# A tile of 128 bytes becomes 256: what stands behind it in SBUF moves from remainder 32 to remainder 160 by 256

## The chip, the cores and the metric

The kernel runs on one core of a Trainium2 chip. The metric is the device time of one execution in microseconds (us), the median of several runs. The profile's span goes from the first to the last instruction of one execution that the hardware profiler recorded.

## What is computed

Two stages. The first is a short convolution over the sequence whose weights come with each token (softmax over 7 taps, 8 heads of 24 channels); the second is a feed-forward layer with ELU between its two products, over 16384 tokens, 192 channels and 2048 inner channels.

```python
w = softmax(weight_gen, axis=-1)                  # [4, 4096, 8, 7]
x_unf = x_pad[:, idx, :].reshape(B, S, 7, 8, 24)  # the token and the 6 before it
x = einsum('bshk,bskhg->bshg', w, x_unf).reshape(16384, 192)
h = x @ w_in                                      # [16384, 2048]
g = where(h > 0, h, exp(min(h, 0)) - 1)
out = g @ w_out                                   # [16384, 192]
```

All is float32. The weights arrive as 64-bit words and are decoded on the chip.

## The kernel before

The 16384 tokens are worked on in 32 blocks of 512. Of each block the convolution is made by GpSimd (products and sums, lines 508 and 524), transposed by VectorE (629), and split into a high and a low part (xhi, xlo; lines 637 and 639), which SyncE's copies also bring to the other half of the partitions (657). Line 473 is the exponential of the softmax; wm and ws (lines 469 to 479) hold its maximum and its sum, 32 numbers a partition each.

The products run on TensorE in fp32r, one pass, with high and low parts. One step is one block and one k of 8, which stands for two tiles of 128 inner channels:

- h = x @ w_in, line 685 (`product_in`): for each of the two tiles nine products, (w high, x high), (w low, x high), (w high, x low) for three thirds of the channels. w_in's tile WI is loaded as weights, 64 partitions by 128 columns, and x's part is the moving stream, 512 columns. The two tiles use the lower and the upper 64 partitions, one instruction each, and run side by side.
- ELU, lines 742, 744, 747, 752, 754: ScalarE and VectorE take h from PSUM and leave its high part hi and its low part lo in SBUF.
- out += g @ w_out, line 713 (`product_out`): here ELU's parts are the weights (64 by 128), and w_out's tile WO is the stream: 384 columns (high and low part) for hi, 192 for lo. Again one instruction for each half of the partitions, side by side. The sums lie in acc and accd in PSUM.

Two steps' products with w_in (36 instructions) stand behind one another, and then two earlier steps' products with w_out (64 instructions). All of block 0 (`plain`) is worked on in plain fp32 in place of that, four passes, straight from the decoded weights m_in and m_out and without low parts; each such matmul stands as two records in the trace. Line 566 sums products of the convolution for blocks 0 and 1 with an identity matrix.

The order of every engine's instructions is fixed by a planner (`Plan`) that has a cost for each task, due times and a table of shifts; it does not know of addresses. TensorE waits for ELU's parts, ELU for h; h has four banks of PSUM, each of which is free again when ELU's last subtraction (754) has read it.

SBUF is filled in the order of first use, each tile at a multiple of 32 bytes. A ring of buffers lies in one piece. In bytes a partition, in the kernel before:

```
start          remainder by 256   tile (buffers x bytes)
16512           128               ident (1 x 512)
17056           160               WI, w_in's parts (1 x 24576)
41632           160               WO, w_out's parts (1 x 24576)
66208           160, 32, 160      wg (3 x 896)
68896            32               xw (3 x 5376)
85024            32               wm (1 x 128)
85152           160               ws (1 x 128)
85280            32               raw_in (3 x 6144), then v, raw_out, pa, pb
132896           32               xhi (2 x 9216)
151328           32               m_in (3 x 3072), then e, m_out
174368           32               hi (7 x 2048)
188704           32               xt (1 x 3072)
191776           32               xlo (2 x 9216)
210208           32               lo (7 x 2048)
224544           32               xc (1 x 3072)
```

Of the kernel before, what the change touches and what calls it, by code (L numbers as in the profile page):

```python
# [52 lines left out]
class Plan:  # L53
# [13 lines left out]
    def add(self, engine, cost, run, reads=(), writes=(), due=None, port=False):  # L67
        t = Task(engine, cost, run, due, port or engine == "pool")
        for h in reads:
            t.needs.update(h.writers)  # L70
        for h in writes:
            t.needs.update(h.users)
            if not h.users:
                if h.make:
                    t.makes.append(h)
                if h.before:
                    t.needs.update(h.before.users)
        for h in (*reads, *writes):
            h.users.append(t)
        for h in writes:  # L80
            h.writers.append(t)
        t.needs.discard(t)
        t.at = len(self.tasks)
        self.tasks.append(t)
        return t
# [50 lines left out]
def conv_elu_kernel(  # L136
# [12 lines left out]
    P, T, HK = weight_gen.shape  # L149
# [7 lines left out]
    H = HK // K // Q  # L157
# [5 lines left out]
    J = N // (A * S)  # L163
# [38 lines left out]
    def rows(ap, t0, n):  # L202

        return ap.rearrange("(a r) t d -> r a t d", r=R)[t0 // T][:, t0 % T:t0 % T + n]

    def quadrants():

        return [(slice((s * Q + q) * A, (s * Q + q + 1) * A), s, q)
                for s in range(S) for q in range(Q)]
# [21 lines left out]
    def ring(name, shape, bufs, dtype=F32, pool=sb):  # L231
        return Ring(pool, shape, dtype, name, bufs)
# [4 lines left out]
    r_m_out = ring("m_out", [P, 2, D], 5, I32)  # L237
    r_xw = ring("xw", [P, HALO + J, DQ], 3)
    r_wg = ring("wg", [P, J, H, K], 3)
    r_wm = ring("wm", [P, J, H, 1], 1)  # L240
    r_ws = ring("ws", [P, J, H, 1], 1)
    r_pa = ring("pa", [P, J, H, G], 2)
    r_pb = ring("pb", [P, J, H, G], 1)
# [26 lines left out]
    def act(cols, psum=False):  # L270
        return cols / 1.2 + (70 if psum else 110)

    def dve(cols):
        return cols / 0.96 + 70
# [9 lines left out]
    def dma(packets, byts):  # L284
        return packets * max(9 + byts / 12, 22) / 20
# [7 lines left out]
    def due1(k):  # L293
        if k < len(FIRST):
            return T0 + FIRST[k]
        return T0 + FIRST[-1] + (k - len(FIRST) + 1) * STEP
# [131 lines left out]
    def chunk(blk):  # L428

        n, t0 = J, blk * J * S  # L430
        xw, wg, wm, ws = r_xw.new(), r_wg.new(), r_wm.new(), r_ws.new()
        wg_h[blk] = wg
        xw_h[blk] = xw
        k, kk = n * H, n * H * K

        def w():
            return wg.t[:, 0:n]

        def wide(h):
            return h.t.to_broadcast([P, n, H, K])  # L440

        def load(to, src, n, d, at=0, both=False, only=quadrants()):
            def run():
                for p, s, q in only:
                    eng = nc.scalar if both and q else nc.sync
                    eng.dma_start(out=to()[p], in_=rows(src, t0 + s * J + at, n)[  # L446
                        :, :, q * d:(q + 1) * d])
            return run

        def load_w(only=quadrants()):  # L450
            return load(lambda: w().rearrange("p t h k -> p t (h k)"), weight_gen, n, H * K,
                        both=blk == 0, only=only)

        if blk == 0:
            add("dma", 700 + Q * S * ISSUE // 2, load_w(), writes=[wg], due=-2)
        for one in quadrants() if blk else ():
            add("dma", max(dma(A * n, H * K * 4), ISSUE), load_w([one]), writes=[wg])
        if blk == 0:
            xw_h[blk] = xw = [xw, Handle()]
            m = n + HALO  # L460
            for i, (a, b) in enumerate(((0, m - JH), (m - JH, m))):
                add("dma", dma(P * (b - a), DQ * 4),
                    load(lambda a=a, b=b: xw[0].t[:, a:b], x, b - a, DQ, a),
                    writes=[xw[i]], due=-1 + i)
        else:
            for one in quadrants():
                add("dma", max(dma(A * (n + HALO), DQ * 4), ISSUE),
                    load(lambda: xw.t, x, n + HALO, DQ, only=[one]), writes=[xw])
        add("dve", dve(kk), lambda: nc.vector.tensor_reduce(
            out=wm.t[:, :, :, 0], in_=w(), axis=AX.X, op=ALU.max), reads=[wg], writes=[wm])  # L470
        add("dve", dve(kk), lambda: nc.vector.tensor_tensor(
            out=w(), in0=w(), in1=wide(wm), op=ALU.subtract), reads=[wm], writes=[wg], port=True)
        add("act", act(kk), lambda: nc.scalar.activation(
            out=w(), in_=w(), func=ACTF.Exp), writes=[wg])
        add("dve", dve(kk), lambda: nc.vector.tensor_reduce(
            out=ws.t[:, :, :, 0], in_=w(), axis=AX.X, op=ALU.add), reads=[wg], writes=[ws])
        add("act", act(k), lambda: nc.scalar.activation(
            out=ws.t, in_=ws.t, func=ACTF.Copy, bias=1e-9), writes=[ws])
        add("dve", 6.4 * k + 60, lambda: nc.vector.reciprocal(out=ws.t, in_=ws.t),
            writes=[ws])  # L480
        if blk == 0:
            wb_h[blk] = [r_h.new(), r_h.new()]
            for i, h in enumerate(wb_h[blk]):
                def half(t, i=i):
                    return t[:, i * JH:(i + 1) * JH]

                def bank(h=h):
                    return h.t[:, 0:kk // 2].rearrange("p (t h k) -> p t h k", h=H, k=K)

                add("dve", dve(kk // 2), lambda half=half, bank=bank: nc.vector.tensor_tensor(  # L490
                    out=bank(), in0=half(w()), in1=half(wide(ws)), op=ALU.mult),
                    reads=[ws, wg], writes=[h], port=True, due=due1(0) - 14000 + 1000 * i)
                if OWN[blk][i] < K:
                    add("act", act(kk // 2, True), lambda half=half, bank=bank: nc.scalar.copy(
                        out=half(w()), in_=bank()), reads=[h], writes=[wg])
            return
        add("dve", dve(kk), lambda: nc.vector.tensor_tensor(  # L497
            out=w(), in0=w(), in1=wide(ws), op=ALU.mult), reads=[ws], writes=[wg], port=True)
# [384 lines left out]
    with tc.manual_schedule():  # L883

        nc.vector.memset(scratch, 0.0)
        add("act", 1500, lambda: nc.scalar.activation(out=scratch, in_=scratch, func=ACTF.Exp),
            due=2500)
        make_identity(nc, ident)
        turn_over(14)
        for s in range(len(todo) + LAG):  # L890
            now = todo[s] if s < len(todo) else None
            up = todo[s - LAG] if s >= LAG else None
            if now:
                blk, k = now
                if k == 0:
                    chunk(blk)
                    if blk < 2:
                        summed(blk, s, OWN[blk])
                    else:
                        conv(blk, s)  # L900
                if blk == 0:
                    if k in in_pieces:
                        weights_in(k, in_pieces[k])
                    weights_out(k)
            period(s, now, up)
            if up and up[1] == NP - 1:
                drain(up[0], s)
        plan.issue()
# [34 lines left out]
```

## Time and profile before

| | |
|---|---|
| median of 3 runs | 1163.75 us (1163.24 to 1163.84) |
| span of the profiled execution | 1161.3 us |
| the profiled execution's own time | not given apart from its span; the median is 2.45 us above it |
| TensorE busy (products) | 1154.9 us, 99% |
| ScalarE, VectorE, GpSimd busy | 913.7, 847.7, 698.3 us |
| granted TensorE clock, mean | 0.999 |
| share of the chain that ended last | PE 98% |

A busy share says that an instruction of the engine was under way, not that the engine ran at its best: products are pipelined, and the start of one and the start of the next say more than the duration of one. The chain that ended last is followed back from the last instruction, at each step to what released it. In the timeline, neighbouring instructions of a kind are merged, and the count stands behind the x; a pair that runs side by side counts as two.

### The profile page before, as it was taken

Reading aid. Unit: us, or ns where it says so; the run is one execution under the profiler, and the core shown is the slowest. Engines: PE = TensorE matmul, PEld = TensorE weight load, DVE = VectorE, ACT = ScalarE, POOL = GpSimd, SP = SyncE. Lnnn points to the kernel's source line nnn. Section 1 sums busy time; section 2 is a strip of 40 time slices with the busy share of each in tenths; the row PEclk is TensorE's granted clock in tenths of the full one; section 3 lists DMA queues with packets and bytes.
Section 4 is the critical chain, followed back from the end, with each engine's and each line's share of the span. In section 5 each row is a group of like instructions: output and inputs, shape, how many; then the busy total and the mean of one; then the engine's idle time right before and its main releaser. Section 6 shows DMA issues by size and latency. Waiting matters only on the chain.

```text
span 1161.3 us, 32341 instructions
## 1 busy us (share of the span) xinstructions
PE 1154.9 (99%) x12844; PEld 1048.7 (90%) x12844; DVE 847.7 (73%) x1502; ACT 913.7 (79%) x1794; POOL 698.3 (60%) x424
## 2 busy tenths in 40 slices
PE   9999999999999999999999999999999999999998
PEld 6699999999989989989999998998999999999997
DVE  7977768776767777777776677776777776777664
ACT  6778778787778878777878777887777887787775
POOL 4666874846687777865557755567755567653000
PEclk9999999999999999999999999999999999999999
DMA  8831322331233232213332223331223321111100
GB/s 194 165 69 43 65 65 67 71 70 43 57 66 74 49 79 54 59 43 69 70 70 49 47 46 70 71 70 40 53 49 70 70 65 35 26 31 42 42 16 15
DMA packets 143127, 71.04 MB, mean 61 GB/s; under 512 B 98816, under 2 KB 141824, under 8 KB 142976
## 3 DMA queue, kind: packets, MB, share of 16 engines
q1 hardware_dynamic: 142112, 68.72, 27.0%
q8 instruction: 101, 1.65, 0.6%
q14 instruction: 50, 0.41, 0.1%
q10 hardware_dynamic: 864, 0.25, 0.1%
HBM read 31.98 MB, written 12.58 MB: 38 GB/s over the span
## 4 chain that ended last, share of the span: by engine, by line
PE 98%; SPq 1%; DMA 0%; ACT 0%; issue 0%; DVE 0%; DVEq 0%; ACTq 0%
PE h L685 46%; PE accd L713 25%; PE acc L713 25%; PE accd L566 0%; PE acc L566 0%; SPq L446 0%; DMA raw_in<-in_moe_w_in 0%; SPq L369 0%; PE h L681 0%; ACT xhi L646 0%; DVE raw_out L867 0%; ACT acc L329 0%; ACT raw_in L332 0%; SPq L404 0%; ACT raw_out L861 0%
## 5 line engine op out<-in xcount | busy, mean ns | idle before, releaser
L747 DVE SCALAR_TENSOR_TENSOR h<-e,h 128x512 f32<-128x512 f32 x496 | 321.8, 693 | 279.8 <-ACT e L744 278.9
L742 ACT ACTIVATE e<-h 128x512 f32<-128x512 f32 x512 | 280.4, 600 | 171.5 <-PE h L685 171.3
L685 PE MATMUL h<-xhi,WI 64*128 64x512 f32 x2976 | 392.5, 394 | 0.0
L754 DVE TENSOR_TENSOR lo<-h,hi 128x512 fp32r<-128x512 f32 x496 | 326.4, 688 | 14.5 <-ACT hi L752 0.7
L752 ACT CAST hi<-h 128x512 fp32r<-128x512 f32 x496 | 290.7, 587 | 53.9 <-DVE h L747 41.2
L685 PEld LDWEIGHTS h<-xhi,WI 64*128 64x128 f32 x2976 | 279.1, 185 | 48.5
L713 PE MATMUL accd<-WO,hi 64*128 64x384 f32 x1984 | 305.9, 357 | 0.0
L713 PE MATMUL acc<-WO,hi 64*128 64x384 f32 x1984 | 304.6, 355 | 0.0
L524 POOL TENSOR_TENSOR pa<-pa,pb 128x768 f32<-128x768 f32 x150 | 289.9, 1932 | 17.0 <-DVE pb L508 5.5
L744 ACT ACTIVATE e<-e 128x512 f32<-128x512 f32 x512 | 297.9, 637 | 0.9
L508 POOL TENSOR_TENSOR pb<-xw,wg 128x768 f32<-128x768 f32 (+1 forms) x179 | 278.0, 1553 | 11.7
L713 PE MATMUL acc<-WO,lo 64*128 64x192 f32 x1984 | 255.6, 249 | 0.0
L713 PE MATMUL accd<-WO,lo 64*128 64x192 f32 x1984 | 254.8, 248 | 0.0
L508 POOL TENSOR_TENSOR pa<-xw,wg 128x768 f32<-128x768 f32 (+1 forms) x31 | 47.2, 1524 | 305.3 <-DVE wg L497 289.3
L685 PE MATMUL h<-xlo,WI 64*128 64x512 f32 x1488 | 214.6, 390 | 0.0
L713 PEld LDWEIGHTS acc<-WO,lo 64*128 64x128 f32 x1984 | 198.5, 187 | 4.6
L713 PEld LDWEIGHTS acc<-WO,hi 64*128 64x128 f32 x1984 | 196.3, 185 | 4.8
L713 PEld LDWEIGHTS accd<-WO,lo 64*128 64x128 f32 x1984 | 198.8, 188 | 0.1
L713 PEld LDWEIGHTS accd<-WO,hi 64*128 64x128 f32 x1984 | 195.1, 184 | 0.1
L685 PEld LDWEIGHTS h<-xlo,WI 64*128 64x128 f32 x1488 | 144.5, 184 | 28.2
L524 POOL TENSOR_TENSOR xc<-pa,pb 128x768 f32<-128x768 f32 x30 | 55.5, 1851 | 2.4
L639 DVE TENSOR_TENSOR xlo<-xt,xhi 128x768 fp32r<-128x768 f32 (+1 forms) x32 | 37.9, 1184 | 1.0
(84 smaller groups left out, 487.1 us busy)
## 6 DMA issues: line engine op xcount, KB each, us to landing
xw<-in_x SPq DMA_DIRECT2D x124, 168.0 KB, 3.5
xhi<-xhi SPq DMA_DIRECT2D x62, 192.0 KB, 3.0
xlo<-xlo SPq DMA_DIRECT2D x62, 192.0 KB, 2.9
out_dram<-raw_out SPq DMA_DIRECT2D x124, 96.0 KB, 1.9
wg<-in_weight_gen SPq DMA_DIRECT2D x126, 28.0 KB, 2.2
raw_out<-in_moe_w_out SPq DMA_DIRECT2D x8, 384.0 KB, 6.2
raw_in<-in_moe_w_in SPq DMA_DIRECT2D x12, 192.0 KB, 5.3
raw_in<-in_moe_w_in SPq DMA_DIRECT2D x8, 96.0 KB, 2.9
```

Of the source, the lines that this page charges most:

```text
L508: lambda: eng.tensor_tensor(out=h.t[:, 0:J], in0=xw.t[:, j0 + k:j0 + k + J, :].rearrange("p j (h g) -> p j h g", g=G), in1=wg.t[:, j0:j0 + ...
L524: add("pool", pool(J * DQ), lambda b=b, to=to: nc.gpsimd.tensor_tensor(out=to.t, in0=a.t, in1=b.t, op=ALU.add), reads=[b] if to is a else ...
L639: add("dve", dve(C * n * A), lambda i=i: nc.vector.tensor_tensor(out=to(xlo, i), in0=xt(i), in1=to(xhi, i).bitcast(F32), op=ALU.subtract), ...
L685: return lambda: nc.tensor.matmul(out=h.t, lhsT=w_in_f[k][1]()[p, c] if w is None else WI[p, k, w, c], rhs=x.t[p, c, c0:c0 + 2].rearrange( ...
L713: return nc.tensor.matmul(out=to(), lhsT=src.t[p, g * P:(g + 1) * P], rhs=w, start=start, stop=False, skip_group_check=True).ins
L742: add("act", act(N, True), lambda: nc.scalar.activation(out=e.t, in_=h.t, func=ACTF.Relu, scale=-1.0), reads=[h], writes=[e])
L744: add("act", act(N), lambda: nc.scalar.activation(out=e.t, in_=e.t, func=ACTF.Exp, scale=-1.0), writes=[e])
L747: add("dve", dve(N), lambda: nc.vector.scalar_tensor_tensor(out=to.t, in0=e.t, scalar=-1.0, in1=h.t, op0=ALU.add, op1=ALU.max), reads=[e, ...
L752: add("act", act(N, True), lambda: nc.scalar.copy(out=hi.t, in_=h.t), reads=[h], writes=[hi])
L754: add("dve", dve(N), lambda: nc.vector.tensor_tensor(out=lo.t, in0=h.t, in1=hi.t.bitcast(F32), op=ALU.subtract), reads=[h, hi], writes=[lo])
```

## The change

The tile wm gets twice the size, and the code uses its first half. All tiles that are placed behind it start 128 bytes later; WI, WO, wg and xw stay. ws stands at 32 then, and raw_in, v, raw_out, pa, pb, xhi, m_in, e, m_out, hi, xt, xlo, lo and xc at 160.

```diff
-    r_wm = ring("wm", [P, J, H, 1], 1)
+    r_wm = ring("wm", [P, 2 * J, H, 1], 1)
...
-        xw, wg, wm, ws = r_xw.new(), r_wg.new(), r_wm.new(), r_ws.new()
+        xw, wg, wm, ws = r_xw.new(), r_wg.new(), r_wm.new(lambda t: t[:, 0:J]), r_ws.new()
```

## Rows read from the trace of the kernel before

**Rows 1.** The page: busy time of the engines; granted clock in 40 slices.

```profile
PE 1154.9 (99%) x12844; PEld 1048.7 (90%) x12844; DVE 847.7 (73%) x1502; ACT 913.7 (79%) x1794; POOL 698.3 (60%) x424
...
PEclk9999999999999999999999999999999999999999
```

**Rows 2.** The page: the chain that ended last, by engine and by line.

```profile
PE 98%; SPq 1%; DMA 0%; ACT 0%; issue 0%; DVE 0%; DVEq 0%; ACTq 0%
PE h L685 46%; PE accd L713 25%; PE acc L713 25%; PE accd L566 0%; PE acc L566 0%; SPq L446 0%; DMA raw_in<-in_moe_w_in 0%; SPq L369 0%; PE h L681 0%; ACT xhi L646 0%; DVE raw_out L867 0%; ACT acc L329 0%; ACT raw_in L332 0%; SPq L404 0%; ACT raw_out L861 0%
```

**Rows 3.** The chain in order of time, 159 to 178 us: start us, us, what.

```profile
159.85 4.21 PE h L685 x36
164.05 1.14 PE acc L713 x16
165.19 1.15 PE accd L713 x16
166.33 1.15 PE acc L713 x16
167.48 1.15 PE accd L713 x16
168.63 4.21 PE h L685 x36
```

**Rows 4.** Timeline of PE, 602.7 to 604.5 us: start us, us, instruction, count.

```profile
602.99 0.34 PE L713 MATMUL acc<-WO,hi 64*128 64x384 f32 x2
603.17 0.25 PE L713 MATMUL acc<-WO,lo 64*128 64x192 f32 x2
603.26 0.36 PE L713 MATMUL acc<-WO,hi 64*128 64x384 f32 x2
603.46 0.25 PE L713 MATMUL acc<-WO,lo 64*128 64x192 f32 x2
```

**Rows 5.** Timeline of the weight loads (PEld), the same stretch.

```profile
603.17 0.19 PEld L713 LDWEIGHTS acc<-WO,hi 64*128 64x128 f32 x2
603.28 0.19 PEld L713 LDWEIGHTS acc<-WO,lo 64*128 64x128 f32 x2
603.46 0.19 PEld L713 LDWEIGHTS acc<-WO,hi 64*128 64x128 f32 x2
```

**Rows 6.** Groups by line, whole span: count, busy us, mean ns, idle before.

```profile
L685 PE MATMUL h<-xhi,WI 64*128 64x512 f32 x2976 | 392.5, 394 | 0.0
L713 PE MATMUL accd<-WO,hi 64*128 64x384 f32 x1984 | 305.9, 357 | 0.0
L713 PE MATMUL acc<-WO,hi 64*128 64x384 f32 x1984 | 304.6, 355 | 0.0
...
L685 PE MATMUL h<-xlo,WI 64*128 64x512 f32 x1488 | 214.6, 390 | 0.0
```

**Rows 7.** Lines 473 and 508: durations in ns, least/median/most; forms.

```profile
L473 ACT ACTIVATE wg<-wg x32: 388/389/424, 4.8 to 1024.6; 128x224 f32<-128x224 f32 x32
...
L508 POOL TENSOR_TENSOR pb<-xw,wg x179: 864/1546/2153, 9.1 to 1051.0; 128x768 f32<-128x768 f32 x177, 128x384 f32<-128x384 f32 x2
...
L508 POOL TENSOR_TENSOR pa<-xw,wg x31: 862/1545/1550, 8.3 to 1031.2; 128x768 f32<-128x768 f32 x30, 128x384 f32<-128x384 f32 x1
```

**Rows 8.** Timelines of DVE, PE and ACT, 607.6 to 612 us.

```profile
607.54 1.35 DVE L754 TENSOR_TENSOR lo<-h,hi 128x512 fp32r<-128x512 f32 x2
...
609.68 0.40 PE L685 MATMUL h<-xhi,WI 64*128 64x512 f32 x2
...
609.88 1.09 ACT L742 ACTIVATE e<-h 128x512 f32<-128x512 f32 x2 [1.72 <-PE h L685]
```

**Rows 9.** Timeline of PE in block 0, 31.6 to 34.6 us.

```profile
31.61 0.32 PE L713 MATMUL accd<-m_out,hi 64*128 64x192 f32 x1
...
31.77 0.32 PE L713 MATMUL accd<-m_out,hi 64*128 64x192 f32 x1
...
31.94 2.74 PE L685 MATMUL h<-xhi,m_in 64*128 64x512 f32 x12
34.51 0.32 PE L713 MATMUL accd<-m_out,hi 64*128 64x192 f32 x1
```

**Rows 10.** Timeline, 602.35 to 602.70 us: stream and next load.

```profile
602.30 0.62 PE L685 MATMUL h<-xlo,WI 64*128 64x512 f32 x4
602.30 0.42 PEld L685 LDWEIGHTS h<-xlo,WI 64*128 64x128 f32 x4
```

## The prediction

> **What bounds the kernel now.** I read the shares of the engines first, then the chain that ended last, then the clock. TensorE is busy for 1154.9 of 1161.3 us, nothing else for more than 913.7, and its granted clock is full, 2.4 GHz of its two levels, in all forty slices [rows 1]. The chain stands on PE for 98% of the span, 46% of it on line 685 and twice 25% on line 713 [rows 2]. So the time is the time that TensorE's own instructions take, and the next view is the same chain in order of time: from 159.85 to 168.63 us one stretch of 36 products with w_in and one of 64 products with w_out take 8.78 us, of which 4.20 are the former and 4.58 the latter, and no other engine stands between them [rows 3]. Since every tile that moves is one that TensorE reads, the question is whether the pace inside these 8.78 us depends on where a tile stands.
>
> How far is that pace from the clock? Products come in pairs, one on each half of the partitions, at the same time. The 36 of line 685 are 18 pairs: 4.20 / 18 = 0.2333 us a pair, where 512 columns at 2.4 GHz take 0.2133. Excess: 20 ns a pair. The 64 of line 713 are 16 times a pair of 384 columns and a pair of 192: 4.58 / 16 = 0.2863 us. The starts show how this is made: the wide pair's weights are loaded while the narrow pair runs, and the next load begins 0.11 us after that one (603.17, 603.28), longer than the 0.08 that 192 columns need; so 0.107 us (128 columns at 1.2 GHz, which the 0.11 fits) plus 0.160 for 384 columns is the floor, and 0.2863 - 0.267 = 19 ns the excess, again one lump for each pair that is not limited by its load [rows 4, 5]. All in all there are (2976 + 1488) / 2 = 2232 pairs of the first kind and (1984 + 1984) / 2 = 1984 wide pairs of the second [rows 6]: 2232 x 20 + 1984 x 19 = 44.6 + 37.7 = 82 us of excess. This is the only thing in the bound that a change of addresses can touch.
>
> **The change part by part.** The tile wm grows from 128 to 256 bytes a partition, and everything that is placed behind it moves up by 128 bytes. Nothing is added, removed or reordered: the view of wm that is used has the old shape, so lines 469 and 471 issue the same instructions, and the planner's costs don't know of addresses. w_in's and w_out's parts stand ahead of wm and stay at remainder 160 by 256, xw and wg stay as well; x's parts (xhi, xlo) and ELU's (hi, lo) go from 32 to 160, and with them e, v, pa, pb, xc, xt and the raw tiles. I cost it in three parts.
>
> *Other engines and the copies: nothing.* The trace holds a test of remainders for ScalarE and GpSimd already: wg's three buffers stand at 160, 32 and 160, used in turn. ScalarE's exponential on them takes 388 ns at the least, 389 in the median, 424 at the most; GpSimd's product of xw (at 32) with wg has medians of 1546 and 1545 ns [rows 7]. If one buffer in three were dearer by tens of ns for all of its uses, a third of the rows would be; the medians cannot show a third, but ScalarE's maximum bounds it at 35 ns. What covers such a cost if it is there: ELU's last subtraction of a step ends at 608.89, and TensorE first writes that bank of PSUM again at 609.68, so 0.79 us of slack, and ScalarE waits 1.72 us for a product in the same round [rows 8]. Without that cover, 35 ns on each of some 1700 ScalarE instructions would be 60 us, but 913.7 + 60 is far below 1161. Copies are off the chain (DMA 0%) [rows 2]. Value taken: 0.
>
> *TensorE's reading where the operands already agree.* In block 0 the products run in plain fp32, and there both operands stand at remainder 32: xhi with m_in, hi with m_out. Each product leaves two records, each for two passes over its columns. Six pairs of records with 512 columns take 34.51 - 31.94 = 2.57 us, 428 ns each against 1024 columns = 426.7; with 192 columns the pitch is 31.77 - 31.61 = 0.16 us against 0.160 [rows 9]. So there the excess is 2 ns a load or less than the rows resolve, although a load runs beside the stream there too. After the change the operands of the fast products agree in the same way. If the remainder is the reason, the whole excess but 2 ns goes: 2232 x 18 + 1984 x 17 = 40.2 + 33.7 = 74 us. If the number format is the reason (one pass in place of four), nothing goes. These are the two ends towards faster.
>
> *TensorE's fast products, worked out.* The estimate between the ends: suppose that a load and a stream hinder each other where they stand at the same remainder by 256. A load of 128 columns (512 bytes a partition) takes 0.107 us; in that time the stream reads 256 columns, 1024 bytes. It gains 512 bytes on the load, two rounds of 256. For the products with w_in both begin at once (the stream at 602.30, the next load at 602.30) [rows 10]. Starting 128 apart, as now, the stream meets the load twice, after gains of 128 and of 384; that makes (20 - 2) / 2 = 9 ns a meeting. Starting 0 apart it meets it once inside, after 256, and stands level with it at the very start and the very end. If these edges cost nothing, one meeting of two goes: 2232 x 9 = 20.1 us. For the wide products with w_out the load begins 0.02 us after the stream (603.26, 603.28) [rows 4, 5], some 200 bytes of lead: from 128 + 200 to 840 it passes 512 and 768, from 200 to 712 it passes 256 and 512. Two before and two after: 0. The sum is -20.1 us, 0.16 us of each round of 8.78, well inside the slack of 0.79, so nothing else becomes late. It is taken against the median of the timed runs: the span is 1161.3 and the median 1163.75, so 2.45 us lie around the span, and stay. 1163.75 - 20.1 = 1143.7 us.
>
> Why this value and not an end: the fp32 rows are the nearest rows with equal remainders, and they speak for a gain; but they differ in format too, and ScalarE and GpSimd show no remainder at all, so I don't take the whole.
>
> Against the change speaks a rule of the Trainium skill, in "SBUF — State Buffer", section "Who interferes with whom": TensorE has two read ports that don't depend on each other, one for the stream and one for the weights, and "PE and ACT never wait on anyone". By it the sum would be 0 and the time 1163.75. The trace agrees that other engines don't disturb TensorE (two rounds in a row take 8.78 us), but of its own two ports it shows nothing either way. The page "TensorE: Matmul & The Clock Gate", section "Wait — 56ns, not 53.3ns?", gives about 2.5 ns over the columns as the fixed cost of a matmul; the fp32 rows agree, the fast rows with their 20 do not, so something is there that this rule leaves unexplained.
>
> **The rivals.** *No change.* The two reads of TensorE don't hinder each other, and the 20 ns belong to the one-pass format. For it: the excess is the same lump for both kinds of product, though the loads begin differently, and the rows of wg show no remainder. Against: nothing in the kernel explains 20 ns. Time: 1163.75. That the change doesn't do what it says falls in here: if the tiles behind wm were placed otherwise, or rounded, the remainders would stay and so would the time.
>
> *Everything goes.* As in fp32: 1163.75 - 74 = 1090. Then a round is 0.6 us shorter, which the slack of 0.79 still covers. Against it: it wants the whole lump to come from one address bit.
>
> *Slower.* The edges count. With equal remainders stream and load begin on the same place at the same time, and end on it: three meetings in place of two for the products with w_in, 2232 x 9 = +20.1 us, 1183.8; if the wide products pay one more as well, 1984 x 9 = 17.9 more, 1201.7. For it: the two begin within the 0.01 us that the rows resolve. Against it: a stream at twice the pace leaves the shared place at once. It decides from the point at which an edge costs more than half a meeting, 4.5 ns.
>
> **How the numbers follow.** Part of the excess goes: 0.34 (its own range 1125 to 1161). Everything goes: 0.08. No change: 0.30. Slower: 0.28, a third of it beyond 1192. Within 0.2% (2.3 us, about what a measurement of this kernel can tell from no change) lies only the third case, so faster 0.42, same 0.30, slower 0.28. The likeliest gives 1143.7. The range from 1108 to 1192 leaves out "everything goes" and the dear end of "slower", 0.08 + 0.09.
>
> **What would show it.** The stretch of 36 products with w_in: 4.04 us if right, 4.20 for no change, 4.36 if the edges count, 3.88 if everything goes. The stretch of 64 with w_out: 4.58 if right, 4.30 if everything goes. Outside these, ELU's instructions keep their means, and the granted clock stays full. The prediction is wrong if the w_in stretch keeps its 4.20, if the w_out stretch moves at all, or if TensorE begins to wait for ELU.

## The result, and the profile after

The changed kernel takes 1151.26 us (median of 4 runs, 1150.74 to 1151.82), the kernel before 1163.80 (median of 4 runs): ratio 0.9893, 95% interval 0.9879 to 0.9907. It is 12.5 us faster; 20.1 were forecast.

The page of the changed kernel: busy times, granted clock, and the chain that ended last.

```profile
PE 1141.9 (99%) x12844; PEld 1034.5 (90%) x12844; DVE 852.2 (74%) x1502; ACT 912.9 (79%) x1794; POOL 698.0 (61%) x424
...
PEclk9999999999999999999999999999999999999999
...
PE 98%; ACT 1%; DVE 1%; SPq 0%; DMA 0%; issue 0%; ACTq 0%; DVEq 0%
```

The picture is the same as before [rows 1, 2]: there are as many instructions, the granted clock is full, and the chain stands on TensorE. Between 100 us and the end's last 6 us, other engines stand on the chain at one place alone: a weight load that begins at 668.7 us has waited 0.5 us for SyncE, and from there the chain is followed back through SyncE's copies and ELU to 655.6 us, while TensorE was at work. TensorE is busy for 13.0 us less, which is about the whole difference. Its pace is what changed. The chain in order of time (start us, us, what):

```profile
159.01 4.15 PE h L685 x36
163.15 1.11 PE acc L713 x16
164.27 1.14 PE accd L713 x16
165.41 1.14 PE acc L713 x16
166.54 1.14 PE accd L713 x16
167.68 4.15 PE h L685 x36
```

Against [rows 3] a round takes 8.67 us in place of 8.78, and both stretches are shorter: the 36 products with w_in 4.15 in place of 4.21, the 64 with w_out 4.53 (163.15 to 167.68) in place of 4.58. The trace keeps starts to the nanosecond; read so, a round is 8.673 = 4.147 + 4.526 us, before 8.780 = 4.206 + 4.574, and the medians over the whole kernel are these same numbers; in both kernels more than nine stretches in ten stay within one or two ns of them. The 2232 pairs with w_in are 124 stretches of 18; 124 x (0.059 + 0.048) = 13.3 us. The span became 12.4 shorter. Most of the rest is in single w_out stretches that are longer than the others, by 1.0 us in all in the changed kernel and 0.3 before (from the starts). In some of them TensorE shows a wait for SyncE's line 700, by which it hands over a bank of PSUM; the kernel before has only the second of these rows (for whom, for what: us, times, longest).

```profile
PEld acc L713 <- SPq L700: 0.7, 2, 0.5
...
PEld accd L713 <- SPq L700: 0.4, 1, 0.4
PE acc L713 <- SPq L700: 0.2, 1, 0.2
```

Two of ELU's groups, which work on moved tiles, first in the kernel before and then in the changed one (busy us, mean ns, idle before):

```profile
L754 DVE TENSOR_TENSOR lo<-h,hi 128x512 fp32r<-128x512 f32 x496 | 326.4, 688 | 14.5 <-ACT hi L752 0.7
L747 DVE SCALAR_TENSOR_TENSOR h<-e,h 128x512 f32<-128x512 f32 x496 | 321.8, 693 | 279.8 <-ACT e L744 278.9
...
L754 DVE TENSOR_TENSOR lo<-h,hi 128x512 fp32r<-128x512 f32 x496 | 326.8, 689 | 14.4 <-ACT hi L752 0.6
L747 DVE SCALAR_TENSOR_TENSOR h<-e,h 128x512 f32<-128x512 f32 x496 | 321.9, 693 | 262.8 <-ACT e L744 261.8
```

The means are 689 and 693 ns where they were 688 and 693, so ELU's work on the moved tiles costs what it did. One smaller group became dearer: the 30 large subtractions of line 639 (xlo) take 1352 ns in place of 1227, 3.8 us in all. The place is not the reason, since they take 1349 ns in e2_both_moved (below), where these tiles stand at 32 again, and TensorE does not wait for them.

Where in a stretch does the gain lie? The timeline of the changed kernel, one stretch of 36 products with w_in (two steps) and the first product behind it:

```profile
609.88 1.57 PE L685 MATMUL h<-xhi,WI 64*128 64x512 f32 x12
611.29 0.86 PE L685 MATMUL h<-xlo,WI 64*128 64x512 f32 x6
611.99 1.53 PE L685 MATMUL h<-xhi,WI 64*128 64x512 f32 x12
613.35 0.84 PE L685 MATMUL h<-xlo,WI 64*128 64x512 f32 x6
614.03 0.33 PE L713 MATMUL acc<-WO,hi 64*128 64x384 f32 x2
```

and one such stretch of the kernel before:

```profile
607.57 1.58 PE L685 MATMUL h<-xhi,WI 64*128 64x512 f32 x12
...
609.68 1.56 PE L685 MATMUL h<-xhi,WI 64*128 64x512 f32 x12
...
611.77 0.34 PE L713 MATMUL acc<-WO,hi 64*128 64x384 f32 x2
```

In the changed kernel the first step's nine pairs take 611.99 - 609.88 = 2.11 us, the second step's 614.03 - 611.99 = 2.04; before, it was 2.11 and 2.09. The two steps are the same amount of work with the same tiles. In the medians, read to the nanosecond, the first step gains 9 ns (2.112 to 2.103 us) and the second 49 (2.093 to 2.044). So the gain is not a fixed amount for each product: it begins after some products, and then a pair takes 2.04 / 9 = 0.227 us, 13 ns over the 0.2133 of its columns.

### The profile page after: what moved, and what is told of

Same layout as the page of the kernel before. It is cut to its first block, busy times and chain, and to the rows that moved or that the text cites. A ratio compares the mean times of both kernels' runs of the same rounds, so it can differ in the third digit from the quotient of the medians.

```text
span 1148.9 us, 32341 instructions
## 1 busy us (share of the span) xinstructions
PE 1141.9 (99%) x12844; PEld 1034.5 (90%) x12844; DVE 852.2 (74%) x1502; ACT 912.9 (79%) x1794; POOL 698.0 (61%) x424
## 4 chain that ended last, share of the span: by engine, by line
PE 98%; ACT 1%; DVE 1%; SPq 0%; DMA 0%; issue 0%; ACTq 0%; DVEq 0%
PE h L685 46%; PE accd L713 25%; PE acc L713 25%; PE acc L566 1%; PE accd L566 1%; PE h L681 0%; DMA wg<-in_weight_gen 0%; SPq L446 0%; ACT hi L752 0%; ACT e L742 0%; SPq L876 0%; DVE raw_out L867 0%; DVE h L747 0%; ACT e L744 0%; ACT xhi L646 0%
## 5 line engine op out<-in xcount | busy, mean ns | idle before, releaser
L685 PE MATMUL h<-xhi,WI 64*128 64x512 f32 x2976 | 387.3, 390 | 0.0
L685 PEld LDWEIGHTS h<-xhi,WI 64*128 64x128 f32 x2976 | 274.7, 184 | 49.6
L713 PEld LDWEIGHTS acc<-WO,hi 64*128 64x128 f32 x1984 | 193.9, 184 | 5.3 <-SPq L700 0.7
L639 DVE TENSOR_TENSOR xlo<-xt,xhi 128x768 fp32r<-128x768 f32 (+1 forms) x32 | 41.7, 1302 | 1.1
```

The source lines that it names most:

```text
L639: add("dve", dve(C * n * A), lambda i=i: nc.vector.tensor_tensor(out=to(xlo, i), in0=xt(i), in1=to(xhi, i).bitcast(F32), op=ALU.subtract), ...
L685: return lambda: nc.tensor.matmul(out=h.t, lhsT=w_in_f[k][1]()[p, c] if w is None else WI[p, k, w, c], rhs=x.t[p, c, c0:c0 + 2].rearrange( ...
L713: return nc.tensor.matmul(out=to(), lhsT=src.t[p, g * P:(g + 1) * P], rhs=w, start=start, stop=False, skip_group_check=True).ins
```

## Experiments

"Level" means that stream and load leave the same remainder by 256. The kernels differ in places of SBUF alone, and each was compared with the kernel before on the same chip; the ratios are to those runs. Where a padding ahead of another ring than wm is needed, the ring takes a tile that nobody uses before its first buffer:

```python
PADS = {'hi': 128, ...}   # bytes ahead of the ring's first buffer
...
            if not self.begun and name in PADS:
                pool.tile([128, PADS[name] // 4], F32, tag=name + "_pad", name=name + "_pad", bufs=1)
```

What came out, with the distance of x's parts from w_in's and of w_out's from ELU's (stream less load, by 256), the stretches as medians of one trace in us, and the ratio to the kernel before with its 95% interval:

```
                     w_in  w_out | stretch  stretch   round | median us  ratio
                     dist   dist |  w_in     w_out          |
before                128    128 |  4.206    4.574    8.780 |  1163.80
changed                 0      0 |  4.147    4.526    8.673 |  1151.26   0.9893 (0.9879 to 0.9907)
e1_w_moved            128    128 |  4.206    4.574    8.780 |  1163.72   1.0000 (0.9991 to 1.0009)
e2_both_moved           0      0 |  4.147    4.526    8.673 |  1150.76   0.9888 (0.9871 to 0.9904)
e3_x_only               0    128 |  4.122    4.572    8.693 |  1153.42   0.9912 (0.9898 to 0.9927)
e4_elu_only           128      0 |  4.217    4.528    8.747 |  1160.70   0.9969 (0.9958 to 0.9980)
e5_pad256             128    128 |  4.206    4.574    8.780 |  1163.87   0.9998 (0.9988 to 1.0008)
e6_pad384               0      0 |  4.147    4.526    8.673 |  1150.88   0.9886 (0.9870 to 0.9903)
e7_pad64              -64    +64 |  4.228    4.532    8.760 |  1161.73   0.9981 (0.9970 to 0.9991)
e8_pad192             +64    -64 |  4.157    4.563    8.720 |  1156.81   0.9937 (0.9918 to 0.9957)
e9_ahead32            +32    +32 |  4.224    4.569    8.793 |  1165.71   1.0016 (1.0007 to 1.0025)
e10_x160_elu96          0    +64 |  4.146    4.561    8.707 |  1154.56   0.9923 (0.9907 to 0.9940)
e11_m_in_off            0      0 |  4.147    4.526    8.673 |  1151.78   0.9896 (0.9876 to 0.9916)
e12_elu96_same512       0    +64 |  4.146    4.561    8.707 |  1154.67   0.9919 (0.9902 to 0.9936)
```

**Agreement, or the place itself?** Theory A: what counts is the distance of the two reads of TensorE by 256. Rival B: what counts is where x's and ELU's parts stand by themselves. Two kernels exchange the places.

```diff
# e1_w_moved; e2_both_moved has the diff of the change besides
-    scratch = const.tile([P, 1], F32, name="scratch")
+    scratch = const.tile([P, 33], F32, name="scratch")[:, 0:1]
```

> The padding stands ahead of w_in's parts: w_in, w_out go to remainder 32, x's and ELU's parts to 160. They differ by 128 as in the kernel before, with the places exchanged. Theory A (what counts is whether stream and load leave the same remainder): a round of two steps stays at 8.78 us, the time at 1164 us, ratio 1.000. Theory B (what counts is where x's and ELU's parts stand by themselves, at 160): round 8.67 us, time 1151 us, ratio 0.989.

> Two paddings of 128 bytes, ahead of w_in's parts and at wm: w_in, w_out at remainder 32 and x's and ELU's parts at 32. Theory A (agreement): round 8.67 us, of which 4.15 for w_in and 4.53 for w_out, time 1151 us, ratio 0.989. Theory B (place of x's and ELU's parts): round 8.78 us, 1164 us, ratio 1.000.

The chain in order of time of e1_w_moved:

```profile
801.54 4.21 PE h L685 x36
805.75 1.14 PE acc L713 x16
...
810.32 4.21 PE h L685 x36
```

and of e2_both_moved:

```profile
801.61 4.15 PE h L685 x36
805.76 1.11 PE acc L713 x16
...
810.29 4.15 PE h L685 x36
```

With all tiles moved and the distance kept at 128, the round keeps its 8.78; with x's and ELU's parts at their old remainder and w_in, w_out brought to it, 8.68 by these rows (8.673 in the table). B has fallen, and with it any story about the other tiles that moved (e, v, the raw tiles) and about other engines' access to them. A timeline of e1_w_moved shows the pace without agreement:

```profile
608.21 1.58 PE L685 MATMUL h<-xhi,WI 64*128 64x512 f32 x12
...
610.32 1.56 PE L685 MATMUL h<-xhi,WI 64*128 64x512 f32 x12
...
612.42 0.34 PE L713 MATMUL acc<-WO,hi 64*128 64x384 f32 x2
```

It is 2.11 us for the first step and 2.10 for the second (2.093 in the median): here the pace of 0.227 never sets in.

**Which product gains?** One half of the change at a time.

```diff
# e3_x_only
+PADS = {'xhi': 128, 'hi': 128, 'xlo': 128, 'lo': 128}
# e4_elu_only
+PADS = {'hi': 128, 'xlo': 128, 'lo': 128}
```

> Only x's parts (xhi, xlo) and the tiles between them and ELU's parts go to 160; ELU's hi and lo stay at 32. Theory A, product by product: the stretch with w_in falls from 4.206 to 4.148 us, that with w_out stays at 4.574, round 8.72, time 1163.8 - 124 x 0.058 = 1156.6 us, ratio 0.994. By the prediction's own model (meetings of stream and load count in the products with w_in alone) the whole of the change's gain would be here: 1151 us, ratio 0.989.

> Only ELU's parts (hi, lo) and xc go to 160; x's parts stay at 32. Theory A, product by product: the stretch with w_in stays at 4.206 us, that with w_out falls from 4.574 to 4.526, round 8.73, time 1163.8 - 124 x 0.048 = 1157.8 us, ratio 0.995. By the prediction's own model nothing: 1164 us, ratio 1.000.

The chain of e3_x_only and of e4_elu_only (with the lines of PADS all lines stand 8 further: 693 is 685, 721 is 713):

```profile
803.83 4.12 PE h L693 x36
807.96 1.13 PE acc L721 x16
...
812.53 4.12 PE h L693 x36
```

```profile
808.32 4.22 PE h L693 x36
812.54 1.11 PE acc L721 x16
...
817.06 2.11 PE h L693 x17
```

Each product gains from its own agreement: with x's parts alone the w_in stretch falls (4.12) and the one with w_out stays (4.57); with ELU's alone it is the other way (4.22 and 4.53). The prediction's own model, by which w_in has the whole gain and w_out none, has fallen in both. But theory A "product by product" missed the sizes as well: the w_in stretch fell further than in the changed kernel (4.122 against 4.147), and rose a little when only ELU's parts moved (4.217 against 4.206). So the stretch ahead may have a say. The timeline of e3_x_only:

```profile
803.67 1.56 PE L693 MATMUL h<-xhi,WI 64*128 64x512 f32 x12
...
805.75 1.52 PE L693 MATMUL h<-xhi,WI 64*128 64x512 f32 x12
...
807.79 0.35 PE L721 MATMUL acc<-WO,hi 64*128 64x384 f32 x2
```

The second step takes the 2.04 us of the changed kernel, the first 2.08 in place of 2.11: the same pace is reached earlier.

That the way in which TensorE enters a stretch decides this shows in the changed kernel itself, with every tile in its place. One of its w_out stretches, with the wait before 668.7 us in it, is 0.48 us longer than the others. Behind it:

```profile
671.08 1.55 PE L685 MATMUL h<-xhi,WI 64*128 64x512 f32 x12
...
673.14 1.52 PE L685 MATMUL h<-xhi,WI 64*128 64x512 f32 x12
...
675.18 0.33 PE L713 MATMUL acc<-WO,hi 64*128 64x384 f32 x2
```

Here the first step takes 2.06 us and the whole stretch 4.108 (to the nanosecond) in place of 4.147. Five full w_out stretches of the changed kernel are longer than the others; behind four of them the w_in stretch takes 4.11 or 4.12 us, behind one 4.15.

**What is the period, and does the distance count gradually?** Other sizes of the one padding at wm.

```diff
# e7_pad64; + 12 in e8_pad192, + 16 in e5_pad256, + 24 in e6_pad384
-    r_wm = ring("wm", [P, J, H, 1], 1)
+    r_wm = ring("wm", [P, J + 4, H, 1], 1)
```

(16 bytes a step of J; the code uses the first J.)

> wm is padded by 256 bytes: x's and ELU's parts stay at remainder 32 by 256, but stand elsewhere by 512 (32 in place of 288; w_in, w_out at 160). If the remainder by 256 is what counts: round 8.78 us, 1164 us. If it is the remainder by 512 or more: another round, and the theory of agreement by 256 falls.

> wm is padded by 384 bytes: x's and ELU's parts agree with w_in and w_out by 512 (160), not only by 256. If 256 is the period: the changed kernel's round, 8.67 us, 1151 us. If the period is 512, so that the change brought the parts half a period apart: less, as for the products with w_in where x's low parts agreed by 512 (4.12 in place of 4.15): 8.65 us or below, 1148 us or below.

> wm is padded by 64 bytes: x's and ELU's parts at 96, 64 away from w_in's and w_out's 160, halfway. If the excess goes gradually with the distance: round 8.73 us, 1157 us. If only agreement counts (by the model of meetings two of them lie inside the load, as at 128): 8.78 us, 1164 us.

> wm is padded by 192 bytes: x's and ELU's parts at 224, 64 beyond 160 on the other side. Gradual in the distance: 8.73 us, 1157 us, as for 64. Only agreement counts: 8.78 us, 1164 us. If 64 and 192 differ from each other, it matters which of the two reads is ahead.

256 bytes give the kernel before to the nanosecond (8.780), and 384 the changed one (8.673). The period is 256. In between, the time does not follow the distance gradually. The chain of e7_pad64 and of e8_pad192:

```profile
808.17 4.23 PE h L685 x36
812.40 1.12 PE acc L713 x16
...
816.93 2.12 PE h L685 x17
```

```profile
805.53 4.16 PE h L685 x36
809.68 1.12 PE acc L713 x16
...
814.25 4.16 PE h L685 x36
```

64 bytes to one side cost the w_in stretch more than 128 do (4.23), to the other side hardly more than level (4.16); for w_out, whose stream stands ahead where the other's stands behind, it is reversed (4.53 and 4.56). That suggested that a stream a little ahead of the load is good.

**A stream a little ahead.** This theory, S, was put to the test at 32 bytes.

```diff
# e9_ahead32
+PADS = {'xhi': 160, 'hi': 192, 'xlo': 64, 'lo': 192}
# e10_x160_elu96
+PADS = {'xhi': 128, 'hi': 192, 'xlo': 64, 'lo': 192}
# e12_elu96_same512
+PADS = {'xhi': 128, 'hi': 192, 'xlo': 64, 'lo': 448}
```

> x's parts go to 192 and ELU's to 128: in both kinds of product the stream stands 32 bytes ahead of the load (x less w_in, w_out less ELU's part). Theory S (it counts how far the stream stands ahead, and a little ahead is at least as good as level: 64 ahead cost little, 64 behind much): w_in 4.15 us or less, w_out 4.53 or less, round 8.67 or less, time 1151 us or less, ratio 0.989 or less. Theory A in its narrow form (level is special): between level and 64 ahead, w_in 4.152, w_out 4.529, 1152 us.

> x's parts at 160, level with w_in's; ELU's at 96, so that w_out's stream stands 64 ahead of them. If the stretch with w_in depends on its own remainders alone: 4.147 us, w_out 4.532, round 8.68, 1152 us. If it depends also on how the stretch before it ends, as when ELU's parts stayed at 32 (w_in 4.122): 4.12 and 4.53, round 8.65, 1149 us, ratio 0.987.

> As the run with x's parts at 160 and ELU's at 96, but ELU's low parts stand 256 bytes further, so that hi and lo agree by 512, as they did in the run with a padding of 64 bytes. There the stretch with w_out took 4.532 us with the same remainders by 256, here 4.561. If the place of lo against hi by 512 makes this difference: w_out 4.532, round 8.68 us, 1151 us. If it is the state in which the stretch with w_in before it ends (x's parts at 96 there, at 160 here): w_out 4.561, round 8.707, 1154.6 us, as without the shift.

The chain of e9_ahead32:

```profile
802.79 4.22 PE h L693 x36
807.02 1.13 PE acc L721 x16
...
811.59 4.22 PE h L693 x36
```

S has fallen: 32 bytes ahead is the slowest place of all that were tried, 1.0016 (1.0007 to 1.0025), although 64 ahead is good. Neither expectation for e10_x160_elu96 came out whole: w_in kept 4.146, as the first had it, but w_out took 4.561, where the same distance had given 4.532 in e7_pad64. e12_elu96_same512 gave 4.561 again, so the place of lo against hi by 512 is not the reason. What is left of the two is that the stretch with w_in ahead of it ends otherwise (x's parts 64 behind there, level here). That is an exclusion; it was not isolated. ELU's high parts also stand at 352 by 512 in e7_pad64 and at 96 in e12_elu96_same512; that a shift by 256 counts for nothing was shown at the distances 128 and 0 alone (e5_pad256, e6_pad384).

**Is the smooth pace of the fp32 products due to agreement?** The prediction leaned on block 0, where plain fp32 products with level operands have hardly any excess.

```diff
# e11_m_in_off: the change, and
+PADS = {'m_in': 128, 'e': 128}
```

> The changed kernel, with m_in alone put back to 32, so that in block 0 the fp32 products of x with the decoded weights read operands 128 apart; all fast products as in the changed kernel. If the small excess of the fp32 products comes from the agreement of the remainders: a record's pitch rises from 429 to about 447 ns. If it comes from the format: 429 ns as before. The time stays at 1151 us either way (84 records).

Its timeline, six pairs of records and the next product:

```profile
28.86 2.74 PE L693 MATMUL h<-xhi,m_in 64*128 64x512 f32 x12
31.43 0.32 PE L721 MATMUL accd<-m_out,hi 64*128 64x192 f32 x1
```

2.57 / 6 = 428 ns with operands 128 apart, the pitch of [rows 9] with level ones. The fp32 products with w_in don't care.

## Why the prediction was right, and where it was not

- *What bounds the kernel, and what alone can change.* Right. The whole difference is in TensorE's pace; the 20 and 19 ns of excess for a pair became 17 and 16 (4.147 / 18 - 0.2133; 4.526 / 16 - 0.267).
- *Other engines and copies at nothing, the order of work untouched, the slack of 0.79 us enough.* Right: ELU's groups kept their means, and TensorE doesn't wait for ELU. Single longer w_out stretches, which the prediction didn't have, took back 0.7 us. Its opening, that every tile that moves is one that TensorE reads, is wrong (e and the raw tiles are not), but e1_w_moved and e2_both_moved show that these don't matter.
- *Stream and load hinder each other by their remainder by 256.* Right, and shown by e1_w_moved, e2_both_moved, e5_pad256 and e6_pad384: exchange both, and nothing happens; bring either to the other, and the gain is there; 256 more, and it is gone.
- *"One meeting of two goes: 2232 x 9 = 20.1 us" and "Two before and two after: 0" for w_out.* This step failed. The products with w_in gave 59 ns a stretch, 3.3 ns a pair or 7.3 us, the ones with w_out, costed at 0, 3.0 ns a pair or 6.0 us. By its own test the prediction was wrong there: the w_out stretch moved, and w_in's was to be 4.04. That the total came as near as it did, 20.1 forecast and 12.5 measured, is luck: one term was too large and the other too small. Nor is the excess one lump for each pair: in the kernel before, the first pair of a w_in stretch takes 0.256 us and the others 0.228 to 0.241 (starts read to the ns). A count of meetings that starts afresh with each product cannot give nearly the whole gain of a stretch to its second step, and it says that 64 to either side are alike, which e7_pad64 and e8_pad192 deny.
- *What the runs put in its place.* The pace depends on the distance and on what went before, as the stretch at 671.08 us shows without any change of places: with level operands the w_in stretch comes, after three pairs in e3_x_only and ten in the changed kernel (starts read to the ns), to 0.227 us a pair and stays there; without agreement it doesn't get there. How stream and load hinder each other in detail stays open; neither distance (e7_pad64, e8_pad192) nor lead (e9_ahead32) orders the results.
- *"If the remainder is the reason, the whole excess but 2 ns goes."* The fp32 rows were no sign of agreement (e11_m_in_off), so that end, 1090 us, had no ground. 13 of the 20 ns stay in the settled pace. Whether they belong to the one-pass format, as the rival "no change" had it for all of them, was not tried.
- *The rule against the change.* By "SBUF — State Buffer" of the Trainium skill, section "Who interferes with whom", TensorE's two read ports are independent and TensorE waits for nobody. The runs differ where its own two reads are concerned: their distance alone makes 8.673 or 8.780 us of a round. With other engines they agree: more than nine stretches in ten keep their length within two ns while these run beside them.

## What to carry to other kernels

Where TensorE's own pace bounds a kernel, read its pitch a product from the starts and compare it with the columns at the granted clock; what is left over can depend on addresses. Then the place of a tile is a parameter like any other: list the remainders by 256 of stream and load, and try level ones first, by a padding at a small tile ahead of them. And a change that resizes a tile moves everything behind it: before a per cent is credited to the change itself, see whether the pitch of products that it doesn't touch has moved.

## What was not expected of the hardware

- A padding of 128 bytes at a tile that TensorE never reads makes 1.1%. The effect is not gradual in the distance: for the stretch with w_in, a stream 32 bytes ahead is nearly the worst (4.224 us), 64 ahead nearly the best (4.157).
- Kernels with the same distances agree to the nanosecond in both stretches (4.206 and 4.574 in three, 4.147 and 4.526 in four), although ScalarE, VectorE, GpSimd and the copies run beside them.
- Equal work on equal tiles runs at two paces in one stretch, 2.10 and 2.04 us a step with level operands (2.11 and 2.09 before), depending on how far the stretch has come; behind a longer w_out stretch the faster pace is there almost from the start (2.06 and 2.04).
